# Gated linear attention and a mixture of experts on one core: idle-column products ahead of the first scores, seven v buffers, y rows stored by ScalarE, dense turned keys, scores between the carried halves

## The chip, the core and the metric

The kernel runs on one core of one Trainium2 chip. The metric is the device time of one execution in microseconds (us), the median of the runs; lower is better. The engines are called PE (TensorE, matrix products), PEld (TensorE loading weights), DVE (VectorE), ACT (ScalarE), POOL (GpSimd) and SP (SyncE, which here only issues DMAs). A trailing q (SPq, PEq) is an engine's sequencer.

## The reference

```python
def _attn_ref(q, k, v, alpha):            # 4 batches, 8 heads, 768 tokens, head size 48
    state = np.zeros((B, H, D, D))
    for t in range(S):
        state = alpha[:, :, t, :, None] * state + np.einsum('bhd,bhe->bhde', k[:, :, t], v[:, :, t])
        y[:, :, t] = np.einsum('bhd,bhde->bhe', q[:, :, t], state)
    return y

def _moe_ref(x, w_gate, w1, w2):          # x: 3072 tokens of 384 values, 8 experts, 1024 hidden values
    logits = x @ w_gate
    # the pairs (token, expert) in falling order of their logits: a token goes to the first of its
    # experts that still has room; an expert takes 3072 / 8 = 384 tokens
    for e in range(E):
        mask = assigned == e
        out[mask] = np.maximum(x[mask] @ w1[e], 0.0) @ w2[e]
    return out
```

The rows of y, heads side by side, are the x of the second part.

## The kernel before, in words

The kernel has three stages: the attention, the choice of an expert for every token (routing), and the experts' two matrix products. The change is in the attention alone; the instructions of the two later stages stand in the same order on every engine in both kernels.

The attention goes by **units**. A unit n (0 to 23) is one chunk of 128 tokens of one batch; `c, b = divmod(n, 4)`, so four units of the same chunk number follow one another, and unit n carries on the state that unit n-4 left. Of a unit's eight heads two lie on one partition range each (48 of 64 partitions), which makes four pairs. In all units but the first and the last, three pairs come in a dense tile of 128 partitions, with the fourth pair packed into the 2 x 16 partitions that are left over; a DMA inside SBUF puts it in its place later (`move`, the tile kq, two DMAs a unit, "k4" in the code).

What one unit does:

- SP issues the loads: `akq` (alpha, k and q together, `loads`) and `v` into a ring of buffers `VR`. Units 0 and 23 have six smaller loads (`whole`) in place of akq.
- DVE scans alpha backwards and forwards (`back`, `fore`), and scales k (`scale_k`, into the tile kq).
- POOL scales q (`scale_q`, into kq). Then SP may issue the two moves of kq.
- PE turns the scaled k (`keys`, three transposes into PSUM), ACT copies them to SBUF (`keys_out`, the tile kn), and PE multiplies them with v (`states`), which DVE adds to the carried state `st`. Units 20 to 23 have no keys and no states.
- PE makes the `scores` (32 small products of the tile kq with itself, in the two halves of the bank pair s), ACT copies them to SBUF (two copies, the tile sm), POOL cuts off what lies above the diagonal (two cuts).
- PE makes y: from the carried state, times the decay that POOL has multiplied in (ms), in two halves (`carried_(1)`, then a two-column ACT copy `tick` that orders them, then `carried_(0)`), and from the unit's own scores and v (`within`). ACT copies y out of PSUM (the tile yta).

Every four units PE makes the gate's logits from yta (`logits`, then a transpose `turned`). The first eight units' y are also turned back to rows in the attention (`tr`, then `y_evict` on ACT into xga) and stored in DRAM by `y_store`, where the experts later gather them. The rest of the y are turned back during routing.

The order of the work on each engine is set by `plan()`: every step is an `op` with an engine, a duration, what it reads and writes and a due time; plan() simulates the engines with these numbers and writes the program in the order that results. Each engine then runs its list strictly in that order, and SP's list is the order of the DMA issues. Rings (`RING`) say how many buffers a tile has: a load into v's buffer n waits until `within` of the unit that had it before has read it. `WARM` steps called `warmer` are products of zeros that write to a spare PSUM tile; plan() puts them where it expects PE to be idle. The constants of the routing stage (INIT and LATE) are made by POOL and DVE during the attention.

The lines of the kernel before that matter: 411 `back`, 416 `fore`, 419 `scale_k`, 423 `scale_q`, 444 keys, 448 keys_out, 461 scores, 468 the copies of the scores, 473 the cuts, 484 states, 493 ms, 496 st, 502 the products of y, 525 tick, 532 the copy of y, 542 logits, 676 the transposes of y, 292 warmer, 389 the moves, 377 the load of akq, 380 the load of v, 648 the store of y, 342 to 354 the late constants on POOL, 357 on DVE.

## Time and profile before

| what | us |
|---|---|
| median of 3 runs (lowest, highest) | 407.96 (407.77, 412.82) |
| the profiled execution | 410.78 |
| its span, first to last instruction | 409.2 |
| of it attention: the last copy of y starts at | 117.57 |
| PE busy over the span | 371.3 (91%) |
| 16 DMA engines, data moved over the span | 87.60 MB, mean 214 GB/s |

Times in the rows are counted from the start of the profiled execution's span, which is 1.58 us shorter than its time. A row with "x16" stands for 16 instructions, and its second number is the time in which at least one of them ran; PE's products overlap, so the duration of one (some 0.25 us) is much longer than its share. "[0.26 <-PE y L502]" is idle time of the engine before the row and what ended it; "issue" is time in which the profile shows nothing that the engine waited for. PEclk is the granted share of TensorE's clock, 1.00 for 2.4 GHz and 0.50 for 1.2 GHz.

### The profile page before, as it was taken

How to read it: one execution, taken by the hardware profiler on the slowest of the kernel's cores; microseconds unless marked ns; L12 is line 12 of the kernel's file. 1: busy time of each engine (PE TensorE's matmuls, PEld its weight loads, DVE VectorE, ACT ScalarE, POOL GpSimd, SP SyncE). 2: the span in 40 equal slices, each digit the busy share in tenths (PEclk: the TensorE clock that was granted, in tenths of full speed). 3: DMA queues.
4: the chain of work that ended last, by engine and by line, in shares of the span. 5: the costliest groups of instructions: out<-in, count | busy, mean ns of one | idle time of the engine just before them, and what ended most of it. 6: DMA issues, size and time to landing. Idle time of an engine off the chain costs nothing.

```text
span 409.2 us, 11538 instructions
## 1 busy us (share of the span) xinstructions
PE 371.3 (91%) x4680; PEld 324.9 (79%) x4680; DVE 243.7 (60%) x687; ACT 166.9 (41%) x323; POOL 174.3 (43%) x270
## 2 busy tenths in 40 slices
PE   6888889979979769999999989999999989999991
PEld 2467768757757559888987979988988989999991
DVE  5756876758626876875865956865966733132110
ACT  3135546546534253155172362353263343553120
POOL 8427768665520131153461551452581473511311
PEclk9559999999998988999999999999999999999998
DMA  8848787895314687479989999889999999995401
GB/s 244 268 140 270 215 266 259 261 284 162 100 62 154 216 307 142 149 172 270 249 284 196 248 290 195 222 296 188 257 311 208 250 272 247 344 280 108 118 11 48
DMA packets 27094, 87.60 MB, mean 214 GB/s; under 512 B 4192, under 2 KB 10912, under 8 KB 27040
## 3 DMA queue, kind: packets, MB, share of 16 engines
q0 software_dynamic: 11712, 56.63, 53.5%
q1 hardware_dynamic: 15328, 30.22, 23.0%
q8 instruction: 37, 0.61, 0.6%
q14 instruction: 17, 0.14, 0.1%
HBM read 75.23 MB, written 9.44 MB: 207 GB/s over the span
## 4 chain that ended last, share of the span: by engine, by line
PE 57%; issue 13%; DVE 10%; DMA 10%; POOL 5%; ACT 3%; POOLq 1%; SPq 1%; ACTq 0%; DVEq 0%
PE h L1129 16%; PE y L1160 13%; PE y L502 6%; DMA wset<-in_w_dram 6%; PE s L461 4%; PE xt L484 3%; PE xt L822 3%; PE xt L444 2%; PE xt L1099 2%; DMA xr<-x_dram,idx 1%; DMA kq<-kq 1%; ACT wset L1064 1%; PE xt L542 1%; PE xt L292 1%; PE xt L803 1%
## 5 line engine op out<-in xcount | busy, mean ns | idle before, releaser
L1160 PE MATMUL y<-wset,hh 128*128 128x384 f32 x384 | 101.7, 346 | 0.0
L1129 PE MATMUL h<-xh,wset 128*128 128x384 f32 x384 | 92.3, 350 | 0.7 <-ACT xh L1104 0.6
L1140 ACT ACTIVATE hh<-h 128x384 fp32r<-128x384 f32 x64 | 31.3, 489 | 104.8 <-PE h L1129 80.2
L1129 PEld LDWEIGHTS h<-xh,wset 128*128 128x128 f32 x384 | 67.9, 192 | 1.5 <-ACT xh L1104 1.4
L1160 PEld LDWEIGHTS y<-wset,hh 128*128 128x128 f32 x384 | 67.4, 189 | 1.6 <-issue 0.9
L1142 DVE SCALAR_TENSOR_TENSOR hl<-h,hh 128x384 fp32r<-128x384 f32 x64 | 35.4, 554 | 53.3 <-ACT hh L1140 45.7
L1160 PE MATMUL y<-wset,hl 128*128 128x384 f32 x192 | 64.8, 337 | 0.0
L1064 ACT ACTIVATE wset<-wset 128x768 fp32r<-128x768 f32 x60 | 47.9, 838 | 22.3 <-DMA wset<-in_w_dram 21.9
L992 POOL DMA_INDIRECT xr<-x_dram,idx x24 | 28.5, 1187 | 51.8 <-DVE key L911 26.3
L1129 PE MATMUL h<-xl,wset 128*128 128x384 f32 x192 | 47.0, 353 | 0.0
L1028 POOL DMA_DIRECT2D wset<-in_w_dram x30 | 18.6, 627 | 60.2 <-DVE sel L901 13.7
L1068 POOL DMA_DIRECT2D wset<-in_w_dram x30 | 28.4, 1205 | 37.4 <-ACT wset L1064 36.4
L473 POOL TENSOR_SCALAR_AFFINE_SELECT sm<-sm 64x512 f32<-64x512 f32 x48 | 31.6, 657 | 26.2 <-ACT sm L468 11.5
L1174 POOL DMA_INDIRECT out_dram<-yo,idx x24 | 26.4, 1101 | 35.8 <-ACT yo L1168 32.2
L1160 PEld LDWEIGHTS y<-wset,hl 128*128 128x128 f32 x192 | 36.0, 188 | 0.0
L1129 PEld LDWEIGHTS h<-xl,wset 128*128 128x128 f32 x192 | 34.0, 193 | 0.5 <-issue 0.3
L840 DVE TENSOR_TENSOR cmp<-nd,iota 128x1536 bf16<-128x1536 bf16 (+4 forms) x32 | 32.7, 1032 | 1.0
L411 DVE TENSOR_TENSOR_SCAN d<-akq,d 128x389 f32<-128x389 f32 x22 | 21.4, 971 | 12.9 <-DMA akq<-in_akq_dram 12.5
L461 PE MATMUL s<-kq 48*64 48x128 f32 (+1 forms) x768 | 24.6, 259 | 3.9 <-POOL kq L423 2.1
L468 ACT ACTIVATE sm<-s 128x384 f32<-128x384 f32 x48 | 21.1, 488 | 17.0 <-PE s L461 12.9
L461 PEld LDWEIGHTS s<-kq 48*64 48x64 f32 x768 | 21.5, 142 | 5.9 <-issue 2.7
L423 POOL TENSOR_TENSOR kq<-akq,ga 128x384 f32<-128x384 f32 x22 | 21.1, 958 | 9.6 <-DVE ga L416 6.1
(185 smaller groups left out, 566.3 us busy)
## 6 DMA issues: line engine op xcount, KB each, us to landing
wset<-in_w_dram POOLq DMA_DIRECT2D x60, 768.0 KB
akq<-in_akq_dram SPq DMA_DIRECT2D x22, 580.5 KB, 5.1
vr<-in_v_dram SPq DMA_DIRECT2D x24, 288.0 KB, 4.6
x_dram<-xga SPq DMA_DIRECT2D x24, 192.0 KB, 1.9
kq<-kq SPq DMA_DIRECT2D x44, 48.2 KB, 3.9
raw<-in_w_dram SPq DMA_DIRECT2D x2, 768.0 KB, 4.8
whole<-in_whole_dram SPq DMA_DIRECT2D x4, 130.0 KB, 3.5
whole<-in_whole_dram SPq DMA_DIRECT2D x4, 129.0 KB, 4.7
```

What stands on the lines that cost most here:

```text
L461: P_.matmul(sps[64 * g:64 * g + half, h, s, cols], kh[hs, 2 * s + g, 1 + half * e:1 + half * e + half], qh[hs, 2 * s + g, half * e:], star ...
L473: G.affine_select(x, x, pattern=[[0, 2 * HP], [1, half]], compare_op=OP.is_ge, fill=0.0, base=0, channel_multiplier=-1)
L502: P_.matmul(yv[64 * s:64 * s + D, g, h, cols], lhs, rhs, start=(g, s) not in fresh, stop=True, skip_group_check=True)
L840: x = op("DVE", (1.75 if nt == 128 else 0.95) * (b - a) / NU + 0.03, lambda js=js: V.tensor_tensor(dense(cbuf[t % 2]) if i > PAIRED and nt ...
L992: gathers[i, b] = op("POOL", 1.15 if b == 0 else 1.0, lambda b=b: nc.gpsimd.indirect_dma_start(out=XR[r2][:, b], out_offset=None, in_=x_dr ...
L1064: pre.append(op("ACT", 0.84, lambda hs=hs: A.activation(WS[i % 2][:, 1, g][:, hs], WS[i % 2][:, 0, g][:, hs].bitcast(F32), AF.Copy, scale= ...
L1068: x = op("POOL", 0.92, lambda: nc.gpsimd.dma_start(WS[i % 2][:, 1, g], w12.bitcast(F32R)[bass.ds(eng_reg[i], 1), :, g].rearrange("e p f -> ...
L1129: P_.matmul(o, WS[i % 2][:, a, g, c0 + d * 128:c0 + (d + 1) * 128], x[:, d], start=m_ == 0 and d == 0, stop=m_ == 2 and d == DB - 1)
L1140: a_ = op("ACT", 0.49, lambda: A.activation(HHT[m], o, AF.Relu), after=[y], r=[("hb", n_)], w=[("hh", n_)], at=at, boost=25, lat=0.1)
L1142: op("DVE", 0.54, lambda: V.scalar_tensor_tensor(HLT[m], o, 0.0, HHT[m], op0=OP.max, op1=OP.subtract), after=[a_], r=[("hb", n_), ("hh", n ...
L1160: P_.matmul(YB[b][:, :Dm], a[:, bs], w, start=q == 0 and n == 0, stop=q == FB - 1 and n == 2)
L1174: st_ = nc.gpsimd.indirect_dma_start(out=out, out_offset=bass.IndirectOffsetOnAxis(ap=IDX[i][:, b:b + 1], axis=0), in_=YO[c % 5], in_offse ...
```

## The change

- `IDLE = (16, 12)`: the scores of unit 0 are issued in two steps, each with a row of products of zeros on 64 columns ahead of it (16 and 12 of them), which write into columns of the scores' bank that nothing reads.
- `WARM` goes from 16 to 2, and a warmer only has to follow the scores of unit 0.
- v has seven buffers in place of five, and its load is due later (n - 1.9 in place of n - 3) and follows the moves of unit n - 2.
- The gate's weights are loaded by ACT's queue, and the y rows of the attention are stored by it too.
- keys_out writes the three turned pairs densely, one after the other, where they were interleaved with a step of three; a second, small copy on ACT collects the fourth pair. states reads the pairs with a step of one.
- The late constants follow the scaling of q of unit 0.
- The scores of unit n+1 are due 0.58 earlier and follow the first carried half of unit n.
- Some durations in plan() change, among them the cost that PE pays for another tile shape.

```diff
+IDLE = (16, 12)
-WARM = 16
+WARM = 2
...
-    RING = dict(akq=5, al=5, k=5, q=5, v=5, sc=1, ...)
+    RING = dict(akq=5, al=5, k=5, q=5, v=7, sc=1, ...)
...
-                o.dur += (0.13 if o.shape != 64 else 0.2) * (o.shape != last_shape)
+                o.dur += (0.2 if 128 in (o.shape, last_shape) else 0.14) * (o.shape != last_shape)
...
-            nc.sync.dma_start(wg[64 * h:64 * h + D, :, :E], ...
+            nc.scalar.dma_start(wg[64 * h:64 * h + D, :, :E], ...
...
-    for i, (e, d_, f) in enumerate(LATE):
-        lates.append(op(e, d_, f, after=lates[-1:], at=9.0 + 0.5 * i if e == "POOL" else 40.0))
+    def constants():
+        last_ = lastw["qh", 0]
+        for i, (e, d_, f) in enumerate(LATE):
+            last_ = [op(e, d_, f, after=last_, at=9.0 + 0.5 * i if e == "POOL" else 40.0)]
...
         op("SP", 0.6, lambda: nc.sync.dma_start(VR[n % RING["v"]]..., v[n]), w=[("v", n)],
-           at=n - 3.0 if n else -1.5, dma=0.87 * slow, lat=1.3)
+           at=n - 1.9, dma=0.87 * slow, lat=1.3, follow=lastw.get(("k4", n - 2), ()))
...
-                if n:
-                    A.activation(keys_, t[0][:, :HG].rearrange("p g r -> p r g"), AF.Copy)
-                else:
-                    A.activation(kn, t[0].rearrange("p g r -> p (g r)"), AF.Copy)
+                A.activation(kn[:, :gs * C], t[0][:, :gs].rearrange("p g r -> p (g r)"), AF.Copy)
+                if gs == HG:
+                    A.activation(
+                        keys_[:, HG].rearrange("p (h x) -> p h x", h=2)[:, :, :D].rearrange("p h (i g) -> p h i g", g=HG),
+                        t[0][:, :HG].rearrange("p g (h x) -> p h x g", h=2)[:, :, D:], AF.Copy)
...
-        op("PE", 0.66, scores, shape=64, ..., at=n + 0.3 - (AHEAD_S if n >= NU - 2 else 0.0))
+        if n == 0:
+            def first_(s):
+                for _ in range(IDLE[s]):
+                    P_.matmul(sps[:, 0, 0, C + half:], warm[:, :128], warm[:, :half], start=True, stop=True)
+                scores((s,))
+            x = op("PE", 0.36 + IDLE[0] * 0.055, lambda: first_(0), ..., after=qs[:1], at=0.3)
+            op("PE", 0.36 + IDLE[1] * 0.055, lambda: first_(1), ..., after=[x], at=0.3)
+        else:
+            op("PE", 0.66, scores, ..., at=n - 0.28, follow=crossed.get(n - 1, ()) if n < NU - 1 else ())
...
-                        lhs = keys_[:, 64 * h:64 * h + D, p] if p < gs else keys_[:, 64 * h + D:64 * h + 64].rearrange(
-                            "p i g -> p (i g)")
-                        P_.matmul(kvp[64 * h:64 * h + D, p], lhs, vr[:, head_], start=True, stop=True)
+                        P_.matmul(kvp[64 * h:64 * h + D, p], keys_[:, p, 64 * h:64 * h + D], vr[:, head_], start=True,
+                                  stop=True)
...
-        nc.sync.dma_start(x_dram..., XG[c % RXG][:, b])
+        q = nc.scalar if n < Y_IN_ATTENTION else nc.sync
+        q.dma_start(x_dram..., XG[c % RXG][:, b])
```

Most of what this does stands in the order that plan() makes of it. The first place is PE from unit 1's states on, in the kernel before (L484 states, L292 warmer, L444 keys, L502 y, L676 the transposes of y, L461 scores; kq_137 is unit 0's tile, kq_138 unit 1's and so on; left out are warmers and the rest of unit 0's y):

```order
L484 MATMUL xt_159<-vr_131,kn_143 48x48 x8
...
L502 MATMUL y<-sm_144,vr_130 48x128 x4
...
L292 MATMUL xt_349<-warm 128x256
L676 MATMUL xt_351<-ident,yta 128x128 x4
L444 MATMUL xt_362<-ident,kq_139 128x128 x3
L484 MATMUL xt_159<-vr_132,kn_142 48x48 x8
L461 MATMUL s<-kq_138 64x128 x4
L461 MATMUL s<-kq_138 64x64 x4
L461 MATMUL s<-kq_138 64x128 x4
L461 MATMUL s<-kq_138 64x64 x4
```

And in the kernel after (L499 states, L449 keys, L518 y, L293 warmer, L694 the transposes of y, L467 scores; kq_139 is unit 0's tile, kq_140 unit 1's):

```order
L499 MATMUL xt_161<-vr_131,kn_145 48x48 x8
L449 MATMUL xt_322<-ident,kq_141 128x128 x3
L518 MATMUL y<-sm_146,vr_130 48x128 x4
...
L499 MATMUL xt_161<-vr_132,kn_144 48x48 x8
L293 LDWEIGHTS warm
L293 MATMUL xt_365<-warm 128x256
L694 MATMUL xt_369<-ident,yta 128x128 x4
L467 MATMUL s<-kq_140 64x128 x4
L467 MATMUL s<-kq_140 64x64 x4
L467 MATMUL s<-kq_140 64x128 x4
L467 MATMUL s<-kq_140 64x64 x4
```

The keys of unit 2 stand ahead of unit 0's y and behind no transposes of y, and one warmer is left of the eleven that stood ahead of unit 1's scores behind unit 0's.

The second place is PE in the middle of the attention, from one unit's states to the next. Before (unit 10's carried halves are on kq_137, unit 11's scores on kq_138, unit 12's keys on kq_139; vr_131 is unit 11's v, vr_130 unit 10's):

```order
L461 MATMUL s<-kq_138 64x128 x4
L461 MATMUL s<-kq_138 64x64 x4
L461 MATMUL s<-kq_138 64x128 x4
L461 MATMUL s<-kq_138 64x64 x4
L484 MATMUL xt_159<-vr_131,kn_143 48x48 x8
L502 MATMUL y<-kq_137,ms_147 48x128 x4
L444 MATMUL xt_1074<-ident,kq_139 128x128 x3
L502 MATMUL y<-kq_137,ms_147 48x128 x4
L502 MATMUL y<-sm_144,vr_130 48x128 x4
```

After (unit 14's carried halves are on kq_143, unit 15's scores on kq_139, unit 16's keys on kq_140; vr_131 is unit 15's v, vr_130 unit 14's):

```order
L449 MATMUL xt_1354<-ident,kq_140 128x128 x3
L499 MATMUL xt_161<-vr_131,kn_145 48x48 x8
L518 MATMUL y<-kq_143,ms_150 48x128 x4
L467 MATMUL s<-kq_139 64x128 x4
L467 MATMUL s<-kq_139 64x64 x4
L467 MATMUL s<-kq_139 64x128 x4
L467 MATMUL s<-kq_139 64x64 x4
L518 MATMUL y<-kq_143,ms_150 48x128 x4
L518 MATMUL y<-sm_146,vr_130 48x128 x4
```

The keys, which stood between the two carried halves, now stand ahead of the states, and the next unit's scores stand between the halves.

The third place is SP's list, the DMA issues, from the moves of unit 1 on. Before (L389 the moves, L377 akq, L380 v, L648 the store of y; vr_130 to vr_134 are the five buffers):

```order
L389 DMA kq_138<-kq_138 48x1x257 x2
L377 DMA akq_126<-in_akq_dram 128x1161
L380 DMA vr_130<-in_v_dram 128x576
L389 DMA kq_139<-kq_139 48x1x257 x2
L377 DMA akq_122<-in_akq_dram 128x1161
L648 DMA x_dram<-xga 128x384
L389 DMA kq_140<-kq_140 48x1x257 x2
L377 DMA akq_123<-in_akq_dram 128x1161
L380 DMA vr_131<-in_v_dram 128x576
```

After (L392 the moves, L380 akq, L383 v; vr_130 to vr_136 are the seven buffers):

```order
L392 DMA kq_140<-kq_140 48x1x257 x2
L380 DMA akq_126<-in_akq_dram 128x1161
L383 DMA vr_133<-in_v_dram 128x576
L392 DMA kq_141<-kq_141 48x1x257 x2
L380 DMA akq_122<-in_akq_dram 128x1161
L383 DMA vr_134<-in_v_dram 128x576
L392 DMA kq_142<-kq_142 48x1x257 x2
L380 DMA akq_123<-in_akq_dram 128x1161
L383 DMA vr_135<-in_v_dram 128x576
```

Before, the v of unit 5 is issued ahead of the moves of unit 2, into the buffer that unit 0 had; after, the v behind the moves of unit 1 is that of unit 3, the first to take a buffer again is that of unit 7, behind the moves of unit 5, and the store of y has left the list.

## Rows read from the trace of the kernel before

**Rows 1.** Timeline of ACT: the copies of y of units 2, 19 and 23.

```profile
33.34 0.60 ACT L532 ACTIVATE yta<-y 128x512 f32<-128x512 f32 x1 [0.51 <-PE y L502]
...
103.09 0.60 ACT L532 ACTIVATE yta<-y 128x512 f32<-128x512 f32 x1 [0.48 <-PE y L502]
...
117.57 0.60 ACT L532 ACTIVATE yta<-y 128x512 f32<-128x512 f32 x1 [1.27 <-PE y L502]
```

**Rows 2.** Windows: length, busy us of PE, PEld, DVE, ACT, POOL; clock, DMA share, GB/s.

```profile
6.00:9.75 3.75, 1.40 (x20) 0.63 (x18) 2.29 (x6) 0.60 (x1) 3.45 (x16) 1.00 1.03 364
9.75:30.23 20.48, 17.38 (x228) 11.97 (x232) 13.19 (x26) 5.05 (x11) 6.66 (x9) 0.50 0.64 213
...
53.00:92.00 39.00, 33.28 (x958) 26.83 (x961) 26.97 (x52) 19.38 (x48) 26.61 (x39) 1.00 0.84 264
92.00:119.00 27.00, 26.24 (x721) 20.42 (x713) 15.74 (x36) 14.91 (x37) 13.45 (x19) 1.00 0.35 108
```

**Rows 3.** Timelines of POOL, DVE and PE in the opening.

```profile
9.03 0.67 POOL L423 TENSOR_TENSOR kq<-whole,ga 128x256 f32<-128x256 f32 x1
...
6.46 0.68 DVE L416 TENSOR_TENSOR_SCAN ga<-whole,d 128x259 f32<-128x259 f32 x1
8.38 0.97 DVE L411 TENSOR_TENSOR_SCAN d<-akq,d 128x389 f32<-128x389 f32 x1 [1.24 <-DMA akq<-in_akq_dram]
...
11.87 1.49 DVE L357 TENSOR_SCALAR iota<-iota 128x512 bf16<-128x512 bf16 x4
...
16.80 2.96 PE L292 MATMUL xt<-warm 128*128 128x256 bf16 x7
```

**Rows 4.** PE's waits from 30 to 92 us: total, times, longest; the longest row.

```profile
PE xt L484 <- issue: 2.7, 2, 2.0
```

**Rows 5.** DMA issues: KB each, median us from issue to landing.

```profile
akq<-in_akq_dram SPq DMA_DIRECT2D x22, 580.5 KB, 5.1
vr<-in_v_dram SPq DMA_DIRECT2D x24, 288.0 KB, 4.6
...
kq<-kq SPq DMA_DIRECT2D x44, 48.2 KB, 3.9
```

**Rows 6.** Timeline of SP: the issue of unit 1's two moves.

```profile
11.77 1.35 SPq L389 DMA_DIRECT2D kq<-kq  x2
```

**Rows 7.** Chain of waits, one unit of the middle.

```profile
67.50 0.63 PE xt L484 x16
68.13 0.37 PE y L502 x8
68.50 0.48 PE xt L444 x3
68.98 1.03 PE y L502 x40
70.01 0.67 PE s L461 x32
```

**Rows 8.** The page's groups: POOL's cuts; busy us, mean ns behind the bar.

```profile
L473 POOL TENSOR_SCALAR_AFFINE_SELECT sm<-sm 64x512 f32<-64x512 f32 x48 | 31.6, 657 | 26.2 <-ACT sm L468 11.5
```

**Rows 9.** ACT's groups in the attention, columns as in rows 8.

```profile
L448 ACT ACTIVATE kn<-xt 128x384 f32<-128x384 f32 x19 | 9.3, 490 | 8.2 <-PE xt L444 8.2
L525 ACT ACTIVATE tick<-y 128x2 f32<-128x2 f32 x20 | 3.5, 173 | 3.2 <-PE y L502 2.0
```

**Rows 10.** One unit's weight loads for states: twelve with step three, last two dense.

```profile
L484 PEld LDWEIGHTS xt<-vr,kn 128*48 128x48 f32 x12 | 0.5, 153 | 0.1
...
L484 PEld LDWEIGHTS xt<-vr,kn 128*48 128x48 f32 x2 | 0.1, 123 | 0.0
```

**Rows 11.** SP's waits: engine and line waited for, us in total, times, longest.

```profile
SPq L380 <- PE y L502: 17.3, 13, 6.7
```

**Rows 12.** Timeline of PE: the warmers in the tail.

```profile
110.45 1.59 PE L292 MATMUL xt<-warm 128*128 128x256 bf16 x5
```

More of the change, by code (lines that the diff above doesn't have):

```diff
@@ L560, in logits @@
         one = len(ns) == 1
-        op("PE", 0.16 if one else 0.64, single if one else lambda: some(ns[0], ns[-1] + 1), shape=32,
+        op("PE", 0.2 if one else 0.82, single if one else lambda: some(ns[0], ns[-1] + 1), shape=32,
            r=[("yt", n) for n in ns] + [("wg", 0)], w=[("LT", g)], banks=("KX",), at=at + 1.0)
@@ L653, in gla_moe_kernel @@
         if n == 0:
+            constants()
             for _ in range(WARM):
-                op("PE", 0.1, warmer, after=lastw["S0", 0], at=60.0, shape=128, clear="T")
+                op("PE", 0.12, warmer, follow=lastw["S0", 0], at=60.0, shape=128, clear="T")
         if n == 2:
-            inits.append(op("DVE", 1.1, lambda: V.tensor_copy(ramp_b, ramp[:, None, :].to_broadcast([128, NU, E])),
+            inits.append(op("DVE", 0.3, lambda: V.tensor_copy(ramp_b, ramp[:, None, :].to_broadcast([128, NU, E])),
                             after=inits + lastw["kh", n], at=7.0))
@@ L689, in gla_moe_kernel @@
                          give="T"))
-        op("SP", 0.1, lambda n=n: y_store(n), after=ev[-1:], at=40.0 + n)
+        op("ACT", 0.3, lambda n=n: y_store(n), after=ev[-1:], at=40.0 + n)
     with tc.manual_schedule():
```

50 lines of the change are left out of this document (27 added, 23 removed).

## The prediction

> **What bounds the kernel now.** I read ACT's copies of y as milestones, then the windows by stage, the chain of waits, and the waits of PE and SP. The rest of the program keeps its order, so what counts is how early the last copy of y comes, now at 117.57 [rows 1]. The attention has three stretches. In the **opening** TensorE ran from 9.75 to 30.23 at a granted clock of 0.50, that is at 1.2 GHz, after a stretch in which it was busy 1.40 of 3.75 us; and it stayed there although it was then busy 17.38 of 20.48 us [rows 2]. The reader should see that part of this was products of zeros, 2.96 us in one piece [rows 3], ahead of unit 1's scores. Unit 2's y is only copied at 33.34. In the **middle**, units 3 to 19, a unit takes (103.09 - 33.34) / 17 = 4.10 us [rows 1]. The window from 53 to 92 holds 39.00 / 4.10 = 9.5 units; a unit there costs PE 33.28 / 9.5 = 3.50 us, DVE 2.84, POOL 2.80 and ACT 2.04, so PE is the fullest, and its idle 0.60 us a unit is mostly of the sort that waits for nothing the profile shows [rows 2, 4]. The loads of a unit, 580.5 + 288.0 + 2 x 48.2 = 965 KB or 0.99 MB, are no bound yet: 264 GB/s at a share of 0.84 is 314 GB/s when full, 3.15 us a unit [rows 2, 5]. In the **tail**, from 92 us on, PE is busy 26.24 of 27.00 us and the DMA share falls to 0.35 [rows 2].
>
> **The opening.** Four edits meet here. POOL scales the second half of unit 0's q at 9.03, though DVE was done with its part at 6.46 + 0.68 = 7.14; POOL was at late constants, which now follow [rows 3]. Of these 1.9 us the idle products may take some, as they stand ahead of the scores on PE. The trace does not show their price: a warmer of 256 columns takes 2.96 / 7 = 0.42 us at 1.2 GHz [rows 3], so for 28 products of a quarter of the columns the bounds are 28 x 0.05 = 1.4 (a quarter of it, at twice the clock) and 28 x 0.42 = 12 (no less than the whole one); I take 1.5, as the columns are what differs most, and it falls in time when PE would wait for POOL and DVE. The scaling of late tables on DVE, 1.49 us just ahead of unit 2's scan [rows 3], moves to places where DVE has slack. And PE's list has unit 1's scores behind one product of zeros, not eleven, and unit 2's keys ahead of the first transposes of y. What then sets unit 2's y is the chain of its own data: DVE starts unit 1 at 8.38, when its load lands, and two units at 2.84 end at 14.1; POOL's product with q, 0.67 x 384 / 256 = 1.0, to 15.1; the two moves, half of 1.35 for the first issue and 3.9 to the landing, to 19.7; scores 0.67, two copies of 384 values at 0.49, two cuts at 0.66, and 32 of the 40 products of y, 0.82, to 23.5 [rows 2, 3, 5 to 9]. Against 33.34 that is **9.8 us** earlier. Taking the gate's weights and a store of y off SP's list costs nothing there: ACT has 4.10 - 2.04 = 2.06 us free a unit [rows 2].
>
> **The clock in the opening.** With the idle products PE is busy more of the stretch after which the clock fell. What follows, up to unit 2's keys, is thin: states and keys of two units, 2 x (0.63 + 0.48) [rows 7]. No row shows what the clock does after such a stretch, so it is open whether it holds. If it falls, a unit's 3.18 us of products [rows 7] grow towards 6.4, for three or four units; half of that lies beside waits for data, so I price it at 5 us, between 0 and 4 x 3.2 = 13. The Trainium skill, "TensorE: Matmul & The Clock Gate", section "Part 1: The HAM clock gate (the "warmup" mystery)", says that sustained activity releases the throttle; by that rule a clock that fell would be back as soon as PE is busy again, the price next to 0 and the time the forecast's. By that rule, the trace does not agree: 20.48 us at 0.50 with PE busy for 17.38 of them [rows 2], so the price stays.
>
> **The middle.** The chain shows a unit as 0.63 (states), 0.37 (first carried half, 8 products), 0.48 (keys), 1.03 (second half and within, 40 products) and 0.67 (scores), 3.18 in all [rows 7]. At the pace of the 40 products, 0.026 each, 8 need 0.21, so 0.16 go where the keys follow the carried half; with the scores there, products of like shape, I count these 0.16 as gone, and 0.05 as new where the keys follow within. The wait for tick between the halves lies under 0.67 of scores where it lay under 0.48 of keys. The dense keys save weight load: twelve loads at 153 ns become like the last ones at 123, and with two side by side that is at most 12 x 0.030 / 2 = 0.18 a unit; I take 0.13, as the products have their own pace [rows 10]. ACT pays with a second copy of 96 values: 0.173 for a copy of two values and (0.490 - 0.173) / 384 = 0.83 ns for each further one give 0.25 us [rows 9], which raises ACT to 2.3 a unit. Keys now run a unit ahead of states, so nobody waits for it; were they back to back, the 0.74 of both copies would stand open in each unit, 19 x 0.74 = 14 us. In sum a unit's 4.10 becomes 4.10 - 0.16 + 0.05 - 0.13 = 3.86; over units 4 to 19, 16 x 0.24, this is **3.8 us**. The bounds: 0, if PE's unexplained idle time takes it back, and 17 x (4.10 - 3.26) = 14 us, if all idle time went and PE's 3.50 - 0.24 were left, just above the loads' 3.15.
>
> **v's buffers.** SP stood 17.3 us waiting until PE had read v, up to 6.7 at a time [rows 11], with moves and loads queued behind it. With seven buffers, and v only two units ahead, this goes. I credit it with nothing in the middle, since PE's idle time there ends on no load; late next is PE itself. What it can give is in the upper bound, and without it the opening's chain would not hold past unit 4.
>
> **The tail.** Four of five warmers go, 4 x 1.59 / 5 = 1.3 us [rows 12]. Eight transposes of y, at 0.48 / 3 each [rows 7], move behind the last within, and four of them stand ahead of the last logits' turn: a net 0.6. Together **1.9 us**, between 0 (the last units wait for POOL instead) and 2.6. The seven later stores on ACT are hidden by its idle 27.00 - 14.91 = 12.09 us [rows 2].
>
> **The sum.** 9.8 + 3.8 + 1.9 = 15.5 us. The profiled execution, 410.78 with a span of 409.2, lies 2.8 above the median; its 410.78 would become 395.3, and the median 407.96 becomes **392.5**.
>
> **The rivals.** (1) The clock falls again in the opening: 392.5 + 5 = 397.5. For it, PE's thin second stretch; against it, the idle products and the shorter waits. (2) PE's idle time in the middle goes with SP's waits: 17 x 0.60 = 10.2 us more, 382; half of it 387. For it, both come while the loads run, and the tail has next to none; against it, the DMA share will rise above 0.84, not fall [rows 2]. The Trainium skill, "Runtime: NRT & Kernel Launch", section "Instruction fetch mechanics", holds that fetching instructions is mostly hidden; by that rule idle time without a releaser has no cause that stays, and the time would be this rival's 382. By that rule, the trace does not agree, with up to 2.0 us at a time [rows 4], which is why this has the smaller chance. (3) The loads become the bound: SP issues akq of unit n+3 behind the moves of unit n, so a ring of three units has to pass two issues (1.35), a landing (5.1), DVE (2.84) and POOL's product, behind two cuts at worst (1.0 to 2.3): 10.3 to 11.6, or 3.4 to 3.9 a unit [rows 2, 5, 6, 8]. That is hardly under 3.86, and PE's next scores now stand ahead of this unit's y and wait for the moves. If fuller DMA engines make the landing 1.5 us longer, a unit takes 4.3: 17 x 0.44 = 7.5 us more, 400. (4) Slower: ACT's stores. A store is issued only when the semaphore that it takes is free, and ACT's other copies stand behind it in a strict list. Four stand in units 18 to 22 and three behind the last copy of y. If each waited as long as an akq takes to land, 5.1 us [rows 5], it would be 7 x 5.1 = 36 us, 428; from 24 / 7 = 3.4 us each the gain turns into a loss of 2%. Against it: most loads are over by then, at a share of 0.35 [rows 2]. That plan()'s order does not come about is no rival: the lists are those of the program.
>
> **How the numbers follow.** Forecast 392.5: 0.48, own range 387 to 397. Rival 1: 0.22. Rival 2: 0.14. Rival 3: 0.12. Rival 4: 0.04. What can be told from no change is some 2%, 8.2 us, so the border is 399.8. Faster: 0.48 + 0.22 + 0.14, less 0.02 for a clock that costs more: 0.82; same 0.14; slower 0.04. The range takes in most of rivals 1 and 2 and the near side of 3: 383 to 402.
>
> **What would show it.** Unit 2's copy of y near 23.5, unit 19's near 89, unit 23's near 102; a granted clock of 1.00 from 10 to 30 us; no long wait of SP for PE's y; states at about 0.50 in the chain and the carried half at 0.21; PE's idle time without a releaser still some 8 us between 23 and 90. If the copies of y of units 4 to 19 come every 3.5 us or less, rival 2 is right, if every 4.2 or more, rival 3; a clock of 0.50 after 13 us is rival 1. The forecast is wrong altogether if unit 2's y is no earlier than 30.

## The result, and the profile after

The changed kernel takes 404.71 us (median of 20 runs, 400.93 to 408.70) where the kernel before, on the same chip and between them, takes 408.29 (405.43 to 412.82): a ratio of 0.9895, 95% interval 0.9863 to 0.9928. That is faster by 1%, no change by the 2% bound; the forecast was 392.5. This ratio and those further down leave out executions that lie more than 1.5% above the fastest of their kernel; the medians leave out none. The profiled execution takes 402.96 with a span of 401.4.

ScalarE's copies of y of units 2, 19 and 23, timeline of the changed kernel (start, length, engine, line):

```profile
28.49 0.60 ACT L548 ACTIVATE yta<-y 128x512 f32<-128x512 f32 x1
...
97.76 0.61 ACT L548 ACTIVATE yta<-y 128x512 f32<-128x512 f32 x1
...
110.43 0.60 ACT L548 ACTIVATE yta<-y 128x512 f32<-128x512 f32 x1 [0.76 <-PE y L518]
```

Against [rows 1] unit 2 is 4.85 us earlier, unit 19 5.33 and unit 23 7.14. From unit 2 to 19 a unit takes (97.76 - 28.49) / 17 = 4.07, where it took 4.10 and 3.86 was forecast. The tail takes 12.67 in place of 14.48. The windows (columns as in [rows 2]):

```profile
6.00:9.75 3.75, 2.62 (x64) 2.03 (x62) 1.40 (x4) 1.30 (x3) 2.39 (x9) 1.00 0.99 334
9.75:13.17 3.42, 1.09 (x19) 0.78 (x19) 3.28 (x5) 0.80 (x3) 0.95 (x2) 0.95 0.95 380
13.17:26.82 13.65, 12.38 (x198) 10.08 (x202) 10.36 (x20) 4.75 (x12) 8.94 (x22) 0.51 0.80 243
...
53.00:92.00 39.00, 31.29 (x986) 26.83 (x985) 26.62 (x50) 20.54 (x58) 25.97 (x38) 1.00 0.83 261
92.00:119.00 27.00, 22.32 (x567) 18.69 (x567) 17.23 (x47) 13.30 (x33) 11.04 (x15) 0.94 0.26 79
```

The idle products filled the first window (2.62 busy in place of 1.40), but the next one is thin, and the clock went to 1.2 GHz at 12.83 all the same; it came back at 26.48, where it had stayed down until 30.23. (The windows are cut 0.34 us later, hence 0.95 and 0.51.) In the middle TensorE has the work that was reckoned: 31.29 / (39.00 / 4.07) = 3.26 us a unit, 0.24 less than before. The unit is no shorter for it: idle time went from 0.60 to 0.81.

One unit in the chain of waits of the changed kernel (start, length), against [rows 7]:

```profile
86.81 0.44 PE y L518 x8
87.25 0.67 PE s L467 x32
87.91 0.88 PE y L518 x40
88.79 0.49 PE xt L499 x16
```

States take 0.49 for 0.63, as forecast. The first carried half, forecast at 0.21, takes 0.44 in this chain, where it comes behind a wait for GpSimd; elsewhere the scores follow it after 0.26. TensorE's waits from 30 to 92 us (total, times, longest), against [rows 4]:

```profile
PE xt L499 <- DVE st L512: 2.5, 2, 1.4
PE y L518 <- issue: 2.1, 4, 1.0
PE xt L499 <- issue: 1.9, 1, 1.9
PE xt L558 <- issue: 1.8, 1, 1.8
PE y L518 <- POOL ms L509: 1.2, 1, 1.2
PE s L467 <- issue: 0.6, 1, 0.6
```

Four of the six rows, 6.4 us, have no releaser. SP's long wait for the reading of v [rows 11] is nearly gone:

```profile
SPq L383 <- PE y L518: 4.8, 4, 1.4
```

### The profile page after: what moved, and what is told of

It is laid out like the page before. It is cut to its first block, busy times and chain, and to the rows that moved or that the text cites. A ratio compares the mean times of both kernels' runs of the same rounds, so it can differ in the third digit from the quotient of the medians.

```text
span 401.4 us, 11589 instructions
## 1 busy us (share of the span) xinstructions
PE 362.6 (90%) x4694; PEld 322.8 (80%) x4694; DVE 244.1 (61%) x687; ACT 168.8 (42%) x342; POOL 175.9 (44%) x270
## 4 chain that ended last, share of the span: by engine, by line
PE 40%; issue 19%; DMA 15%; POOL 11%; DVE 8%; ACT 3%; POOLq 1%; SPq 1%; ACTq 0%; DVEq 0%
PE h L1147 13%; DMA wset<-in_w_dram 11%; PE y L1178 11%; POOL sm L490 4%; PE y L518 3%; DMA akq<-in_akq_dram 3%; PE s L467 3%; POOL kq L428 2%; POOL out_dram L1192 2%; PE xt L840 2%; POOL xr L1010 1%; PE h L762 1%; PE xt L1117 1%; PE xt L499 1%; DMA xr<-x_dram,idx 1%
## 5 line engine op out<-in xcount | busy, mean ns | idle before, releaser
L1147 PE MATMUL h<-xh,wset 128*128 128x384 f32 x384 | 91.3, 347 | 0.8 <-ACT xh L1122 0.6
L1147 PEld LDWEIGHTS h<-xh,wset 128*128 128x128 f32 x384 | 67.0, 189 | 1.6 <-ACT xh L1122 1.4
L1147 PE MATMUL h<-xl,wset 128*128 128x384 f32 x192 | 46.1, 348 | 0.0
L518 PE MATMUL y<-sm,vr 64*48 64x128 f32 (+1 forms) x768 | 23.1, 253 | 2.2 <-issue 2.1
L467 PE MATMUL s<-kq 48*64 48x64 f32 (+1 forms) x768 | 23.0, 255 | 2.2 <-issue 2.2
L467 PEld LDWEIGHTS s<-kq 48*64 48x64 f32 x768 | 21.2, 140 | 3.6 <-issue 2.9
```

What stands on the lines that cost most here:

```text
L467: P_.matmul(sps[64 * g:64 * g + half, h, s, cols], kh[hs, 2 * s + g, 1 + half * e:1 + half * e + half], qh[hs, 2 * s + g, half * e:], star ...
L518: P_.matmul(yv[64 * s:64 * s + D, g, h, cols], lhs, rhs, start=(g, s) not in fresh, stop=True, skip_group_check=True)
L1147: P_.matmul(o, WS[i % 2][:, a, g, c0 + d * 128:c0 + (d + 1) * 128], x[:, d], start=m_ == 0 and d == 0, stop=m_ == 2 and d == DB - 1)
```

## The experiments

The kernels ran in five groups, each on a chip of its own and beside runs of the kernel before, whose medians were 413.28, 411.92, 411.97, 414.27 and 410.59 us, more than beside the changed kernel. So the changed kernel ran once more in the third group (c_after), and ratios are compared with its 0.9806 as well as with 0.9895. These are ratios of the same two kernels, 0.9% or 3.7 us apart, and their intervals do not meet; so a difference of that size between kernels of different groups tells nothing, and where it can be done a kernel is compared within its group. plan() orders the work anew for every kernel. GpSimd, VectorE and ScalarE keep the changed kernel's order in e_hold, e_fill, e_nomove, e_nov and but for the one edited load in e_wg; in e_lead4, e_lead4y, e_best and the a_ kernels they do not. The last columns are the copies of y of units 2, 19 and 23 in the one profiled execution.

| kernel | group | median | ratio to before, interval | u2 | u19 | u23 |
|---|---|---|---|---|---|---|
| e_hold | 1 | 404.88 | 0.9882 (0.981 to 0.995) | 28.52 | 97.02 | 109.68 |
| e_wg | 1 | 404.97 | 0.9856 (0.978 to 0.993) | 26.74 | 97.57 | 110.08 |
| e_ms | 1 | 402.52 | 0.9791 (0.972 to 0.986) | 28.25 | 98.41 | 111.22 |
| e_nomove | 1 | 399.70 | 0.9671 (0.959 to 0.975) | 27.97 | 92.15 | 104.81 |
| e_lead4 | 2 | 406.44 | 0.9821 (0.977 to 0.987) | 26.45 | 98.80 | 113.95 |
| e_open | 2 | 404.24 | 0.9828 (0.977 to 0.989) | 28.76 | 99.34 | 111.96 |
| e_fill | 2 | 407.09 | 0.9896 (0.986 to 0.993) | 26.60 | 105.21 | 117.88 |
| b_mid | 2 | 410.81 | 0.9970 (0.994 to 1.001) | 31.49 | 103.54 | 118.38 |
| c_after | 3 | 404.30 | 0.9806 (0.975 to 0.986) | 26.67 | 97.42 | 110.08 |
| e_nov | 3 | 399.75 | 0.9633 (0.957 to 0.970) | 28.53 | 92.13 | 104.79 |
| e_ysp | 3 | 403.17 | 0.9773 (0.972 to 0.982) | 28.74 | 97.75 | 110.75 |
| e_best | 3 | 403.18 | 0.9776 (0.972 to 0.984) | 30.20 | 92.54 | 105.06 |
| b_v7 | 4 | 411.40 | 0.9945 (0.987 to 1.002) | 30.54 | 98.54 | 113.74 |
| a_v5 | 4 | 405.95 | 0.9829 (0.968 to 0.998) | 25.75 | 95.43 | 109.30 |
| a_nomid | 4 | 404.68 | 0.9875 (0.980 to 0.995) | 29.70 | 100.61 | 113.34 |
| e_lead4y | 4 | 409.95 | 0.9991 (0.994 to 1.004) | 28.94 | 100.83 | 116.14 |
| a_open | 5 | 401.59 | 0.9779 (0.973 to 0.983) | 29.70 | 96.99 | 109.84 |
| e_msy | 5 | 399.90 | 0.9702 (0.964 to 0.976) | 27.46 | 96.05 | 108.57 |

**The opening: clock or data.** e_hold adds rows of products of zeros ahead of ten steps for which TensorE waited:

```diff
+HOLD = {("st", 0): 28, ("kn", 1): 12, ("st", 1): 40, ("kn", 2): 10, ("y", 0): 16, ("st", 2): 24, ("sc", 1): 30,
+        ("kn", 3): 10, ("st", 3): 24, ("sc", 2): 24}
```

> The changed kernel, and 218 more products of zeros on 64 columns in the opening (units 0 to 3), each row of them ahead of a step for which TensorE waited in the trace of after; nothing else moves. Theory A, the clock: after 13.17 us TensorE stood at 0.50 until 26.82, and its list, not the chain of the data, set unit 2's y at 28.49. With the products the clock stays at 1.00; unit 2's y comes near 25.0, and the whole is 3 to 4 us shorter than the changed kernel, ratio to before near 0.981. Rival B, the data: unit 1's loads come 1.1 us later than before and the moves take 4 us to land; the clock is 1.00, but unit 2's y stays at 27.5 to 28.5 and the ratio at 0.988 to 0.990.

The clock held, in the windows and the copy of unit 2's y:

```profile
9.75:13.17 3.42, 3.12 (x90) 2.86 (x86) 3.28 (x7) 1.51 (x4) 1.20 (x3) 1.00 0.88 352
13.17:26.82 13.65, 11.74 (x337) 10.28 (x337) 10.96 (x22) 4.43 (x11) 8.85 (x22) 1.00 0.80 250
```
```profile
28.52 0.60 ACT L558 ACTIVATE yta<-y 128x512 f32<-128x512 f32 x1
```

Unit 2's y comes where it came at half the clock, and the time does not move. But this does not price the clock, since the added rows are work themselves. Unit 2's moves landed at 20.33, and in the 3.23 us until its scores start two rows of 24 products take 1.7 (TensorE, timeline of e_hold):

```profile
21.47 0.86 PE L402 MATMUL s<-warm 128*128 128x64 bf16 x24 [0.60 <-ACT sm L493]
22.26 0.56 PE L508 MATMUL xt<-vr,kn 128*48 128x48 f32 x16
22.76 0.87 PE L402 MATMUL s<-warm 128*128 128x64 bf16 x24
23.56 0.90 PE L475 MATMUL s<-kq 48*64 48x128 f32 x32
```

The changed kernel's second profile tells more, because there the same program had its clock back sooner. In c_after it was at 1.2 GHz from 12.73 to 19.56 alone (window, and the copy of unit 2's y):

```profile
13.17:26.82 13.65, 11.57 (x264) 9.39 (x266) 11.13 (x23) 6.03 (x16) 10.41 (x25) 0.77 0.76 240
```
```profile
26.67 0.60 ACT L548 ACTIVATE yta<-y 128x512 f32<-128x512 f32 x1 [0.55 <-PE y L518]
```

Unit 2's y comes 1.82 us sooner than in the first profile, though its moves landed later, at 21.33 for 20.67. In these two executions the clock is thus worth some 1.8 us at unit 2, by theory A's mechanism; at unit 19 they are 0.34 apart, and what it is worth to the whole is not shown. The rival, that the first loads set unit 2's y, was to be tested by the next two. In e_wg the gate's weights go out behind unit 0's keys; in e_open v of two units and the gate's weights stand again between akq of unit 1 and of unit 2.

```diff
-    op("ACT", 0.9, wgate_load, after=[c_wg, c_pad], w=[("wg", 0)], at=WG_AT, lat=3.0)
+                op("ACT", 0.9, wgate_load, after=[c_wg, c_pad, ko], w=[("wg", 0)], at=n + 0.45, lat=3.0)   # e_wg
+    op("SP", 0.87, wgate_load, after=[c_wg], w=[("wg", 0)], at=WG_AT, dma=1.0, lat=1.0)                    # e_open
-           at=n - 1.9, dma=0.87 * slow, ...
+           at=n - 1.9 if n > 1 else -1.5, dma=0.87 * slow, ...                                              # e_open
```

> The changed kernel, with the two loads of the gate's weights issued by ScalarE behind unit 0's keys in place of ahead of them, so that they no longer travel among unit 1's loads. Rival B of the opening, the data: akq of unit 1 lands near 8.3 in place of 9.375, every step of units 1 and 2 moves 1.1 us to the front, ratio near 0.987. Theory A, the clock: the load lands earlier, but TensorE's list at the lower clock sets unit 2's y, which gains 0.5 us or less; ratio 0.988 to 0.990.

> The changed kernel with v of units 0 and 1 and the gate's weights back on SP's list between akq of unit 1 and akq of unit 2, as before. Theory A: akq of unit 2 and 3 are issued later and no longer share the DMA engines with that of unit 1, which lands near 8.3 in place of 9.4; the moves of unit 1 are issued near 12 in place of 13.19, and with them the whole loop of the loads runs 1.1 us earlier, to unit 19's y near 96.6; 1 us off the whole, ratio 0.986 to 0.988. Rival B: akq of unit 1 lands earlier, but what comes later is set by TensorE, and unit 19's y stays within 0.5 us of 97.76.

Both missed: akq of unit 1 landed at 9.88 and 9.72, no earlier than 9.38, so they did not test what an earlier landing would bring. Against the rival speaks that it landed later in c_after (9.53) and e_wg than in the first profile, and unit 2's y came 1.8 us sooner in both. The 8.29 of the kernel before was that execution's; b_mid, with the same list of loads, had 9.53. The times of e_wg and e_open are those of the changed kernel within the intervals.

**The parts of the change.** b_mid puts only the two edits of the middle (dense keys with the second copy, scores between the halves) on the kernel before; a_nomid takes them out of the changed one. b_v7 and a_v5 do the same with v's seven buffers and late loads. a_open keeps neither: the opening, the tail and ScalarE's queue alone.

```diff
-    RING = dict(akq=5, al=5, k=5, q=5, v=7, sc=1, ...)
+    RING = dict(akq=5, al=5, k=5, q=5, v=5, sc=1, ...)
-           at=n - 1.9, dma=0.87 * slow, lat=1.3, follow=lastw.get(("k4", n - 2), ()))
+           at=n - 3.0 if n else -1.5, dma=0.87 * slow, lat=1.3)
```

> The kernel before with only two edits of the change: the dense keys with the second copy, and the next unit's scores between the carried halves (with the durations in the planner that belong to them). The forecast's term for the middle: 3.8 us less, ratio 0.991. Theory A, the loop of the loads: from unit 7 to unit 19 the loads of the kernel before came every 3.76 us, which these edits don't touch; no gain, ratio 0.997 to 1.003. If TensorE's idle time grows by what its work shrinks, the same.

> The changed kernel without its two edits of the middle (keys interleaved again, one copy; scores where they were). The forecast's term: 3.8 us more than the changed kernel, unit 19's y near 101.5. Theory A: TensorE has slack, as the 12 added products a unit showed, so at most 1 us, unit 19's y at 97 to 98.5.

> The kernel before with one part of the change: seven buffers of v, loaded two units ahead behind the moves. The forecast gave this part nothing. Theory A, the loop of the loads: in the kernel before akq of unit 7 was issued at 32.30 (25.48 after), since v's wait for TensorE stands in SP's list ahead of the moves and the next akq; without it akq of unit 7 goes out near 27, that of unit 19 near 73, unit 19's y comes near 98.5 in place of 103.09, and this part alone has most of the change's gain: 3 to 5 us, ratio 0.987 to 0.992. Rival, the opening on TensorE (idle products, tables, warmers) is what brought the 5 us: unit 19's y within 1 us of 103, ratio 0.997 to 1.003.

> The changed kernel with v's five buffers and early loads back, all other edits kept. Theory A: SP waits again for TensorE to have read v, akq of unit 19 is issued near 76 in place of 72, unit 19's y comes at 101 to 103; 3 to 5 us more than the changed kernel. Rival, the rest of the change carries the gain: unit 19's y at 97 to 98.5, no change beside the changed kernel.

> The kernel before with the edits of the opening, of the tail and of ScalarE's queue alone (idle products, two warmers, late constants behind q, gate's weights and y rows on ScalarE); v's five buffers, the interleaved keys and the old place of the scores stay. If opening and tail carry the change's gain, as the changed kernel without v's buffers (405.95) and without the middle's edits (404.68) say together: 404 to 406, ratio 0.977 to 0.985 on a chip where the kernel before takes 412. If instead either of v and the middle is needed and each stands in for the other: 408 to 410, ratio 0.99 to 0.996.

> The changed kernel once more, as the measure for the three that run on the same chip: ratio to before 0.986 to 0.993, as in its own timing (0.9895).

c_after missed: 0.9806 where 0.986 to 0.993 was expected. The middle's edits are worth 1.2 us on the kernel before (0.9970 of 411.92; between nothing and 2.7), and in the changed one the times show nothing. Only a_nomid's profile, of an execution 2.6 us above its median, has unit 19's y at 100.61, near the forecast's 101.5 and not at theory A's 97 to 98.5. v's buffers brought unit 19's y to 98.54 as theory A had it, but in time 2 to 3 us (0.9945, and the medians) that are not clear of nothing; and without them the changed kernel is no slower as far as an interval of 0.968 to 0.998 can tell, with unit 19's y at 95.43, so that theory's expectation for a_v5 missed. a_open has, as far as two groups can be compared, all of the gain, 0.9779 beside c_after's 0.9806, although SP waits for the reading of v nearly as before:

```profile
SPq L383 <- PE y L518: 15.6, 9, 3.9
```
```profile
96.99 0.60 ACT L548 ACTIVATE yta<-y 128x512 f32<-128x512 f32 x1 [0.23 <-PE y L518]
```

**What the middle waits for.** First TensorE's own work, made longer, with 12 products of zeros ahead of the scores of units 4 to 19:

```diff
+            for _ in range(FILL if 3 < n < 20 else 0):
+                P_.matmul(sps[:, 0, 0, C + half:], warm[:, :128], warm[:, :half], start=True, stop=True)
```

> The changed kernel with 12 products of zeros on 64 columns ahead of the scores of units 4 to 19, 0.47 us a unit at the pace of the 12 in the opening, 7.5 us in all. Theory A, another loop than TensorE's sets the pace: TensorE is idle 0.7 us a unit and takes most of this in; the whole is 0 to 3 us longer than the changed kernel, ratio 0.99 to 0.997. Rival B, TensorE's list is the bound: nearly all of it shows, 6 to 8 us, ratio 1.004 to 1.009.

By the ratios 0.9896 / 0.9806 makes 3.7 us of the 7.5 added; beside e_open, of the same group, it is 2.8, by ratios as by medians: half or less, and with the intervals anything from nothing to 6. The one profile says otherwise: unit 19's y comes 7.45 us later than in the changed kernel's first profile, as much as was added; this execution, at 413.14, was the second longest of ten, 6 us above the median. So TensorE is no idle bystander; that it is not the whole bound is what the times say. Then the DMAs. e_nomove does not move the fourth pair, e_nov does not load v from unit 7 on, e_lead4 issues akq a unit further ahead, e_lead4y does that with the stores of y on SP.

```diff
-                nc.sync.dma_start(dst, src)
+                return src                                                        # e_nomove
-        op("SP", 0.6, lambda: nc.sync.dma_start(VR..., v[n]), w=[("v", n)],
+        op("SP", 0.6, lambda: nc.sync.dma_start(VR..., v[n]) if n < 7 else None, w=[("v", n)],   # e_nov
-    CK, LEAD, WHOLE = C1 + C, 3, (0, NU - 1)
+    CK, LEAD, WHOLE = C1 + C, 4, (0, NU - 1)                                      # e_lead4, e_lead4y
-        q = nc.scalar if n < Y_IN_ATTENTION else nc.sync
-        q.dma_start(
+        nc.sync.dma_start(                                                        # e_ysp, e_lead4y, e_best, e_msy
```

> The changed kernel without the moves of the fourth pair: its 48 rows of keys and q are zero, so a part of scores, states and y is left out; every engine but the DMA queue keeps its list. Theory A, the ring through GpSimd: it loses 1.25 us of issue and 1.5 to 3 us of landing in two units, so the next bound is reached, TensorE's own 3.3 or the loads' 3.15: a unit takes 3.4 to 3.6, 8 to 11 us less in the middle, and unit 2's y comes 2 us earlier; ratio 0.96 to 0.97. Rival B, idle time of TensorE without a releaser: the moves are hidden, a unit takes 3.9 to 4.1, ratio 0.985 to 0.99.

> The changed kernel without the loads of v from unit 7 on (288 KB of a unit's 965 KB; these units take the v of earlier ones, so that part of the result is left out). Theory A, the loop of the loads, whose longest piece is the landing of akq and of the moves among other transfers: with three tenths of the traffic gone an akq lands 1 to 1.5 us earlier and the moves too, a round of three units falls from 11.7 to about 9.5 us, a unit of the middle takes 3.4 to 3.6, ratio 0.965 to 0.975. Rival B, the strict lists of GpSimd, ScalarE and TensorE: landing times are hidden, ratio 0.985 to 0.99. Besides: if TensorE's idle time without a releaser comes from the transfers, it falls below half of its 8.0 us (26 to 98 us) here; if not, it stays.

> The changed kernel, with akq of unit n+4 in place of n+3 issued behind the moves of unit n (that of unit 4 behind unit 1's keys); the five buffers stay. Theory A, the loop of the loads: in the trace of after an akq is issued behind two moves, lands 3.5 to 6.5 us later, goes through VectorE (2.7) and GpSimd (0.95 and its list), and only then come the moves that free the next issue: 10.9 to 12.8 us for three units, 3.6 to 4.3 a unit, which takes back what TensorE saves. With four units in a round it is 2.8 to 3.2 a unit: VectorE no longer waits for akq, unit 19's y comes 3 to 5 us earlier than 97.76, ratio to before near 0.98. Rival B, TensorE: its list with the idle time that has no releaser sets the pace; loads come earlier and nothing else moves, unit 19's y at 97 to 98, ratio 0.988 to 0.991.

> The changed kernel with akq a unit further ahead and the stores of y on SP, the product of state and total left on GpSimd. Theory A: it is the lead that brought unit 19's y to 92.5 in the kernel with four edits; here 92 to 94.5, and the end of the attention 3 to 5 us earlier than 110.4. Rival C, a loop through GpSimd (product with q, moves, scores, copies, cuts, product of state and total) that a longer lead does not touch: 96.5 to 98, and it was the move to VectorE that counted.

Less to move or to load helps: 0.9671 and 0.9633, some 5 us beside e_hold and e_wg or beside c_after, of the same groups, by the medians and more by the ratios, unit 19's y at 92.1 in both. The pace of 3.78 and 3.74 a unit falls short of theory A (3.4 to 3.6); the gain is more than its rivals allow (a ratio of 0.985 or above). Both kernels leave out a part of the result. The side question of e_nov gets no answer: TensorE's idle time without a releaser from 26 to 98 us is 4.5 us there, but also 4.5 in c_after, which is the changed kernel with all its transfers.

A longer lead should have loosened theory A's loop of the loads, and VectorE no longer waited right behind each akq: in e_lead4y it started 2.1 us after the landing in the mean of units 7 to 19, 0.74 in the changed kernel. Yet e_lead4y is the slowest of the changed kernels, 4 to 5 us over a_v5 and a_nomid of the same group by the medians. (e_lead4, at 0.9821 and 406.44, doesn't tell on which side it is.) The lead is not the only difference, though: plan() also wrote other lists for TensorE, VectorE and ScalarE, and the tail takes 15.3 us where it took 12.67. So the loop of the loads is not refuted by it. The data in e_lead4y waited for TensorE: the copies of scores began 8.5 us after the moves had landed, in the mean of units 7 to 19, where the changed kernel has 3.8. And TensorE's clock was lower, 0.87 for 1.00 in this window:

```profile
53.00:92.00 39.00, 34.65 (x914) 29.45 (x915) 28.20 (x52) 18.56 (x52) 21.78 (x33) 0.87 0.72 225
```

Last the lists of GpSimd and ScalarE: the product of state and total on VectorE (e_ms), the stores of y on SP (e_ysp), both (e_msy), and both with the longer lead and the loads of e_open (e_best).

```diff
-            e = V if n >= NU - 2 else G
+            e = V
```

> The changed kernel, with the product of state and total of every unit on VectorE in place of GpSimd; plan() swaps keys and states on TensorE in some units as well. Theory A for the middle, a ring through GpSimd: the product with q of unit n, two moves, their landing, scores, two copies, two cuts, the product of state and total, the product with q of unit n+2. In the trace of after that ring is what is never slack; it loses 0.5 us in two units, so a unit of the middle takes 3.8 in place of 4.07, the whole is some 4 us shorter than the changed kernel, ratio near 0.98. Rival B, TensorE's idle time without a releaser takes back what its own list saves: GpSimd has nothing to do with it, a unit stays at 4.0 to 4.1, ratio 0.988 to 0.991.

> The changed kernel with the y rows of the attention stored by SP again. In the trace with the product on VectorE ScalarE stood 5 us ahead of a store, its copies behind it, and 2.7 us in the one with v back between the loads; in the trace of after no store waits. Forecast's rival 4: if stores on ScalarE cost in most executions, this kernel is 2 to 4 us shorter than the changed one, ratio 0.980 to 0.985. Otherwise SP's list, which is the loop of the loads, gets seven issues more: ratio 0.989 to 0.993.

> Four edits together on the changed kernel: akq a unit further ahead, the product of state and total on VectorE, v of units 0 and 1 and the gate's weights back between the first akq loads, the stores of y on SP. Theory A: the first loosens the loop of the loads, the second shortens GpSimd's part of it, so they relieve one loop and add up only until TensorE's own 3.3 a unit and its idle time are left: 3.7 a unit, 6 to 8 us less than the changed kernel, ratio 0.970 to 0.976. Rival: each of them only removes waits that some other list puts back; ratio 0.979 to 0.983, as with the single edits.

> The changed kernel with the product of state and total on VectorE and the stores of y on SP, akq three units ahead as before. In the trace with the first edit alone the landing of the moves was followed by the copies of scores after 1.9 us in place of 3.8 and one store on ScalarE cost 5 us. If GpSimd's list is what the middle waits for: unit 19's y at 93 to 95 and 399 to 401 in all, less than every kernel so far. If many lists of nearly equal length share the bound, as the kernels so far suggest: 401 to 404.

In e_ms's profile, timeline of ScalarE, a store waits 5 us with the copies of scores behind it:

```profile
88.21 0.17 ACT L541 ACTIVATE tick<-y 128x2 f32<-128x2 f32 x1
93.43 0.35 ACTq L665 DMA_DIRECT2D x_dram<-xga  x1
93.88 0.49 ACT L485 ACTIVATE sm<-s 128x384 f32<-128x384 f32 x1 [5.50 <-DMA vr<-in_v_dram]
```

e_ysp alone gains 1 us by the medians, less than can be told. e_ms is 2.4 us below e_hold and e_wg of its group by the medians, with intervals that overlap. e_best missed what was expected of it: four edits give no more than single ones in time, though its profile ends the attention 5 us earlier than the changed kernel's, at 3.67 us a unit in the middle. e_msy is the shortest kernel that leaves nothing out: 399.90, ratio 0.9702, below the changed kernel's first interval; but a_open, on the same chip, takes 401.59, and their intervals overlap. The time was as expected, the place was not: 96.05 for unit 19's y, in an execution of 402.39. The copies of scores begin 2.5 us after the moves have landed, in the mean of units 7 to 19 (e_ms 1.9), where c_after has 3.6; but a_open, which leaves the product on GpSimd, has 2.0. That GpSimd's list is a part of what the middle waits for is thus likely from the times, and not shown.

## Why the prediction was wrong

**The opening, 9.8.** The step that failed is "What then sets unit 2's y is the chain of its own data". Its copy came at 28.49 where 23.5 was reckoned. TensorE in the opening of the changed kernel, timeline:

```profile
18.18 1.08 PE L694 MATMUL xt<-ident,yta 128*128 128x128 f32 x4
19.19 1.56 PE L467 MATMUL s<-kq 48*64 48x128 f32 x32
20.68 0.90 PE L449 MATMUL xt<-ident,kq 128*128 128x128 f32 x3
22.16 0.88 PE L499 MATMUL xt<-vr,kn 128*48 128x48 f32 x16 [0.58 <-ACT kn L452]
22.97 1.56 PE L467 MATMUL s<-kq 48*64 48x128 f32 x32
24.30 1.50 PE L518 MATMUL y<-sm,vr 64*48 64x128 f32 x32
25.74 0.89 PE L449 MATMUL xt<-ident,kq 128*128 128x128 f32 x3
26.56 0.90 PE L467 MATMUL s<-kq 48*64 48x128 f32 x32
```

Of the 5.0 us too many, 1.0 is the landing of unit 2's moves, at 20.67 for the 19.7 reckoned, because unit 1's akq came 1.1 us later than in the one execution that I took it from. Then 2.3 pass until its scores start at 22.97, behind unit 1's scores and two other steps of the strict list. The last 1.7 lie between scores and copy, 5.5 for the 3.8 reckoned: the products run at half the clock, and the y stands behind unit 1's y, unit 4's keys and unit 3's scores. In c_after, with the clock back at 19.56, the three are 1.6, 0.9 and 0.6. I had laid that list before the reader and then summed the data alone. The 33.34 that it was set against was one execution's too: b_mid and b_v7, which keep the warmers and the late constants as they were, have 31.49 and 30.54.

The second fault is the sum itself: it hands the opening's gain on whole to a middle of fixed pace. In the changed kernel, c_after, e_hold, e_wg, e_ysp and a_open unit 2's y comes between 26.67 and 29.70, and unit 19's between 96.99 and 97.76 in all six, with no order between the two (e_open, 28.76, has 99.34 after a store on ScalarE that TensorE waited 2.7 us for; a_v5, 25.75, has 95.43). The changed kernel and e_wg from unit 2's y to unit 19's, with the clock at 1.00 throughout in both:

```profile
28.49:97.76 69.27, 57.10 (x1789) 48.83 (x1789) 51.30 (x98) 37.85 (x104) 47.00 (x69) 1.00 0.82 252
```
```profile
26.74:97.57 70.83, 57.58 (x1789) 48.98 (x1787) 51.20 (x97) 37.80 (x105) 47.70 (x70) 1.00 0.81 255
```

The middle that began 1.75 us sooner took 1.56 longer; the lead was gone by unit 5's y. Measured at unit 19, in one execution of each, opening and tail edits alone brought 103.09 - 96.99 = 6.1 us.

**The clock.** The event of rival 1 came about, with a chance of 0.22. Its price of 5 us is not measured: e_hold shows only that rows of added products which hold the clock up gain nothing, and c_after that a clock which is back 6.9 us sooner brings 1.8 us at unit 2 and 0.3 at unit 19, which may be chance.

**The middle, 3.8.** TensorE's work shrank as worked out, to 3.26 us a unit, and little came of it: b_mid puts the term at 1.2 us, between nothing and 2.7, and a_nomid shows none in time. The step that failed is reading the fullest engine as the bound, so that what it is spared is time saved. At 0.85 busy it was the fullest, but what it was spared went into waiting, 0.81 us a unit for 0.60. I had put the bound 0 down to idle time without a releaser. That did not grow: it is 7.6 us from 26 to 98 us before, 8.0 after and 4.5 in c_after. The waits that grew have releasers, VectorE's state and GpSimd's product, 3.7 us together, 4.8 in c_after.

The idle time without a releaser has a pattern that I overlooked. Counted along TensorE's list, products and weight loads together, the pauses behind unit 2 stand 256 instructions or a multiple of that apart, within one: at 1730, 1987, 2242, 2498, 3010, 3267, 3523 and 4034 in the changed kernel, at 2755, 3010 and 3523 in c_after, and at 962, 1219, 1731, 1987, 2243, 3010, 3266 and 3523 before. So a pause can fall inside one operation's row; instruction 3523, in the changed kernel and in c_after, and a queue that moved instructions, from the changed kernel's DMA view (packets, MB, share of 16 engines):

```profile
81.58 1.07 PE L558 MATMUL xt<-yta,wg 128*32 128x128 f32 x28 [1.80 <-issue]
```
```profile
82.60 1.07 PE L558 MATMUL xt<-yta,wg 128*32 128x128 f32 x28 [2.35 <-issue]
```
```profile
q8 instruction: 37, 0.61, 0.6%
```

37 packets beside TensorE's 9462 products and weight loads are one for 256. The pauses thus fit borders between blocks of the program that are loaded as it runs; no run changes that loading, so it is not proven. Rival 2 fell, as idle time did not go with SP's waits; the Trainium skill's rule behind it ("Runtime: NRT & Kernel Launch", section "Instruction fetch mechanics", fetching mostly hidden) does not agree with the trace if that is what these 8.0 us are.

**Rival 3.** At 4.07 a unit the middle lay between the forecast and the 4.2 that was to prove it. The DMA share, which was to rise above 0.84, is 0.83. Whether its loop through SP sets the pace is open: less to move or to load brought the unit to 3.74 and 3.78, and the kernel with a longer lead was slower, but with other lists as well.

**v's buffers, 0.** Right in the changed kernel: a_v5 and a_open are as fast without them, as far as the intervals tell, with 15 us of SP's waits back. On the kernel before b_v7 leaves 2 to 3 us possible.

**The tail, 1.9.** Right: 12.67 for 14.48, 1.8 us; the kernels without the tail's edits took 14.8 and 15.2, those with them 12.5 to 13.9, but for e_lead4 and e_lead4y (15.2 and 15.3).

**Rival 4.** The mechanism exists, 5 us once in e_ms. What it costs in the mean is not clear of nothing, 1 us by e_ysp's median, and not 36.

**From the attention to the whole.** "The rest of the program keeps its order" is true, but it does not keep its time. From unit 23's y to the end it took 291.6 us before and 290.9 after, and 289.3 to 296.5 in the other profiles. The profiled execution of before lies 2.5 us above its median, that of after 1.7 below: so 7.8 between the two profiles is 3.6 between the medians. In group 3 the same two kernels are 7.7 apart. What the whole gained is therefore 4 to 8 us, against the 15.5 of the sum: from single profiles some 6 for 9.8 and 1.8 for 1.9, from the times 0 to 1.2 for 3.8.

What stays open is what sets the pace of the middle. Fewer moves and less to load help by 5 us and more; a shorter list on GpSimd may, by 2 to 4 us that are not clear of the noise; less work on TensorE brought 1.2 us of 3.8, and an earlier load was not tested alone. Several lists of nearly the same length fit all of this, and no run isolates one.

## What to carry to other kernels

Before work on the fullest engine is priced, make it longer on purpose: TensorE, 80% busy in the changed kernel, took 7.5 us more and the times showed about 3, though one profile showed all of it. Work that is added to hold a clock up is work too: two executions of the same kernel with different clocks told more than such rows. A gain at the start of a pipeline is worth what it is still worth at its last stage, so read it there. A start time that hangs on a DMA's landing should be taken from more than one execution. And idle time that has no releaser is worth counting out in instructions, not only in microseconds.

## What the runs showed of the hardware

The same first load, unit 1's akq behind the same list, landed at 8.29 us in one kernel's profile and at 9.53 in another's (before, b_mid). TensorE's pauses without a releaser in the middle, up to 2.4 us in the three profiles counted, stand 256 of its instructions apart or a multiple of that. The clock, once at 1.2 GHz, came back after 13.65 us with TensorE busy for 12.04 of them; in the same program's second profile after 6.83 us, 5.55 of them busy. And the program behind the last copy of y, whose lists are the same in all kernels, took TensorE longer where the clock was lower; from that copy to the end in e_open and in a_v5:

```profile
111.96:401.30 289.34, 267.80 (x2208) 245.38 (x2207) 166.50 (x532) 112.68 (x197) 102.77 (x132) 0.99 0.81 215
```
```profile
109.30:405.70 296.40, 274.37 (x2208) 250.89 (x2208) 166.53 (x532) 112.85 (x197) 104.64 (x133) 0.95 0.80 210
```

The same 2208 products kept TensorE busy 6.6 us longer at a mean granted clock of 0.95 for 0.99, and the stretch took 7.1 us more. That is as much as the whole change gained.
